# Pair products handed to TensorE beside the chain's stages, transposed in place: a linear-attention scan with a MoE on one core

## The chip, the cores and the metric

One core of a Trainium2 chip runs the whole program in one launch. The metric is the time of one execution on the device in microseconds; the kernel before was timed in three runs. A profile is of one more execution.

## What is computed

The reference is a recurrence over 768 steps for 32 heads (4 batches of 8) with a 40 x 40 state, whose output goes through a two-layer network:

```python
for t in range(S):
    y[:, :, t] = np.einsum('bhd,bhde->bhe', rt, state)
    Sa = np.einsum('bhde,bhe->bhd', state, at)
    state = state * wt[..., None] - np.einsum('bhd,bhe->bhde', Sa, bt) + np.einsum('bhd,bhe->bhde', vt, kt)
x = y.transpose(0, 2, 1, 3).reshape(3072, 320)
h = x @ w_in                       # 320 x 2048
g = np.where(h >= 1, h, np.where(h <= -1, 0.0, (h + 1) ** 2 / 4))
out = g @ w_out                    # 2048 x 320
```

All of it is in float32.

## The kernel before, in words

The scan is done in 24 chunks of 32 steps, with all 32 heads at once, in two half-batches of 16 heads (`hb`). Four chunks make a set, so there are six sets, 0 to 5. A chunk needs four things that don't depend on the state: decayed rows of k, a and b (the preparation, key `rows`, function `prelude`, L241), the products of the rows of a with the rows of b in the chunk, 32 x 32 for each head (the pair products, key `ab`, function `ab_set`, L312), the inverse of a triangular matrix made of these (key `inv`, function `invert`, L348, 31 steps of two GpSimd instructions), and score products (L478). The chain (`chain`, L504) then takes the state through the chunk, in four stages: products L519; products L529 with the inverse; products L545 and L556; products L585. Each stage is evicted by ScalarE or VectorE before the next can run.

Behind the chain the MoE (`moe`, L628) works on groups of 64 steps: products L637 (first layer), a gate on ScalarE and VectorE (L647 to L653) with a remainder on GpSimd (L654), products L668 (second layer).

The schedule is manual: each engine runs its instructions in the order in which this program issues them. A chunk has four slots. In each, the stages of the chain that are due are issued first (stage 3 of one half-batch and stage 1 of the next in the first and third slot; stage 4, stage 2 and then scores in the second and fourth), and then `fill` (L917) is called. `fill` makes six steps; in each it issues MoE work (`feed`, L901), then weight conversion, then background work (`background`, L411). The position `now` grows by 2.5 per slot, so by 10 per chunk: chunk c begins at position 10 c.

Background work is `rows`, `ab` and `inv` of the next sets. Each is a Python generator that issues some instructions and yields a number of budget units. `WINDOWS` (L28) gives from and to which position a set is worked on. `background` spreads the set's size (a sum of its yields) over its window, with the first of each two slots getting 1.4 shares and the second 0.6 (`SHARE`, L37), and advances the generator until the units spent reach the share. When a window of `inv` begins, `drain` issues what is left of the set's `ab`. Sets 0 and 1 are made in another way at the start; the generator does sets 2 to 5.

`ab_set` works on a chunk of rows in `tiab` (or, in set 2, by turns in a part of `lw` and `tiab`). `load_rows` (L298, DMAs at L304 on SP's queue) fetches it from DRAM; `shift_rows` (L306, two ScalarE copies, L310) moves the last 8 of 40 columns to other partitions; VectorE transposes 32 x 32 blocks into a tile `ea` of 8 head pairs, that is half of the chunk (L325, two instructions per half); TensorE makes 16 products for this half (L336), each recorded as two instructions; ScalarE copies the 128 x 128 result from PSUM to `pairs` (L343). `AB_W` (L41) holds the units yielded behind these steps: 6 behind the shift, 26 ahead of the products, 6 ahead of the copy, 3 behind it, 8 between chunks and 30 behind a first load. The next chunk's load is issued behind the second half's transposes. `psum()` gives one of four PSUM buffers, which the chain, the scores and the pair products share: a first write to one waits for the last eviction from it.

Of the kernel before, what the change touches and what calls it, by code (L numbers as in the profile page):

```python
# [9 lines left out]
F32 = mybir.dt.float32  # L10
# [13 lines left out]
O_R, O_V, O_K, O_P, O_A, O_B = 0, 40, 80, 120, 160, 200  # L24
# [2 lines left out]

WINDOWS = dict(  # L28
    rows=[(0, 0), (24, 43), (46, 64), (70, 90), (106, 130)],
    ab=[(0, 0), (44, 55), (68, 84), (95, 119), (135, 159)],  # L30
    inv=[(2, 28), (55.5, 79), (85, 118), (121, 158), (161, 198)],
)

# [4 lines left out]
SLOTS = len(SHARE)  # L38

ROWS_W = (2, 2, 4, 2, 6, 6, 8)  # L40
AB_W = (6, 26, 6, 3, 8, 30)  # L41
INV_W = 12
INV_STEP = [0.45 + (j + 1) * (31 - j) / 256 for j in range(31)]

# [11 lines left out]
def rwkv_moe_kernel(ctx: ExitStack, tc: tile.TileContext, r, k, v, w, a, b, w_in, w_out, ident_d, mask_d, out):  # L56
    nc = tc.nc
# [10 lines left out]
    psum = lambda: psa.tile([128, 512], F32, tag="p2", name="p2", bufs=4)  # L68
# [29 lines left out]
    work = ctx.enter_context(tc.tile_pool(name="work", bufs=1))  # L98
# [14 lines left out]
    pairs_f = pairs.rearrange("p m i -> p (m i)")  # L113
# [184 lines left out]
    def load_rows(dst, c, off, n, h0=0, nh=NH):  # L298

        sc = scr[c // 4]  # L300
        for f in range(2):
            row = (h0 + f) * 128 + 32 * (c % 4)
            src = bass.AP(sc.tensor, sc.offset + row * RW + off, [[RW, 32], [256 * RW, nh // 2], [1, n]])
            nc.sync.dma_start(dst[64 * f : 64 * f + 32], src)  # L304
# [7 lines left out]
    def ab_set(s):  # L312

        bufs = [lw[:, 0:1280].rearrange("p (h x) -> p h x", x=80), tiab] if s == 2 else [tiab]
        for c in range(4 * s, 4 * s + len(bufs)):
            load_rows(bufs[c % len(bufs)], c, O_A, 80)
            yield AB_W[5]
        for c in range(4 * s, 4 * s + 4):
            shift_rows(bufs[c % len(bufs)])
            yield AB_W[0]  # L320
            tv = bufs[c % len(bufs)].rearrange("p h (j x) -> p h j x", x=40)[:, :, :, 0:32]
            for half in range(2):
                ea = work.tile([128, 8, 2, 32], F32, tag="ea", name="ea")
                for i in range(2):
                    nc.vector.transpose(ea[:, 4 * i : 4 * i + 4], tv[:, 8 * half + 4 * i : 8 * half + 4 * i + 4])  # L325
                    yield 1
                if half and c + len(bufs) < 4 * s + 4:
                    load_rows(bufs[c % len(bufs)], c + len(bufs), O_A, 80)
                yield AB_W[1]
                ps = psum()[:, 0:128]  # L330
                for p in range(8):
                    for f in range(2):
                        rows = slice(64 * f, 64 * f + D)
                        q = 2 * f + p % 2
                        sl = p // 2
                        nc.tensor.matmul(  # L336
                            ps[32 * q : 32 * q + 32, 32 * sl : 32 * sl + 32],
                            lhsT=ea[rows, p, 0, :], rhs=ea[rows, p, 1, :], start=True, stop=True,
                        )
                yield AB_W[2]  # L340
                assert s - 1 in turned_in
                at = 256 * (c % 4) + 128 * half
                nc.scalar.copy(pairs_f[:, at : at + 128], ps)  # L343
                yield AB_W[3]
            if c < 4 * s + 3 and len(bufs) == 1:
                yield AB_W[4]

    def invert(s):  # L348

# [22 lines left out]
    def adopt(s):  # L372
# [3 lines left out]
        nc.vector.transpose(tinv.rearrange("p c h i -> p i (c h)"), W.rearrange("p (a i) -> p i a", i=32))  # L376
        turned_out.add(s)

    def staged(key, needs, work_of):
        for s in range(2 if key != "inv" else 0, NS):  # L380
            if needs:
                drain(needs, s)
            total = 0
            for d in work_of(s):
                total += d
                yield d
            if s:
                size[key] = total
            done[key] = s
            yield 0  # L390

    turned_in, turned_out = set(), set()
    done, size, spent = dict(rows=1, ab=1), dict(rows=10 + 4 * (1 + sum(ROWS_W)), ab=2 * AB_W[5] + 4 * AB_W[0] + 8 * (2 + sum(AB_W[1:4])), inv=INV_W + 2 * sum(INV_STEP)), {}
    back = {k: staged(*a) for k, a in dict(
        rows=("rows", None, prelude), ab=("ab", "rows", ab_set), inv=("inv", "ab", invert)).items()}

    def drain(key, s):

        while done.get(key, -1) < s:
            next(back[key])  # L400
# [464 lines left out]
    at = lambda n, f: todo.setdefault(n, []).append(f)  # L865
# [17 lines left out]
    i = 0  # L883
# [27 lines left out]
    def catch_up():  # L911

        for f in deferred:
            f()
        deferred.clear()

    def fill():  # L917

        catch_up()
        for k in range(6):  # L920
            feed(1280)
            if first:
                first.pop(0)()
            due[0] += PACE[now[0] >= 20]
            while due[0] > 0:
                pull(wgen)
                due[0] -= 1
            background(now[0] + 10 / SLOTS * (k + 1) / 6)
        now[0] += 10 / SLOTS
# [89 lines left out]
```

## Time and profile before

| | |
|---|---|
| median of 3 runs | 791.98 us (785.94 to 795.64) |
| the profiled execution | 791.32 us |
| its span in the trace | 789.5 us |
| busy: TensorE, VectorE, ScalarE, GpSimd | 680.1, 590.6, 472.6, 449.7 us |
| mean granted clock of TensorE | 0.907 |

The span reaches from the first instruction of the program to the last. TensorE has two rows: PE for products, PEld for weight loads, which overlap. DVE is VectorE, ACT ScalarE, POOL GpSimd, SP the engine that issues most DMAs. A line such as L336 is a line of the kernel above. The granted clock is the share of full speed that the chip let TensorE have; 1.00 and 0.50 are the two levels seen.

### The profile page before, as it was taken

To read this page: it belongs to the slowest core of one execution; us is meant where nothing else is said; L and a number is where in the kernel's file an instruction comes from. 1 tells how busy PE (TensorE), PEld (TensorE's weight loads), DVE (VectorE), ACT (ScalarE), POOL (GpSimd) and SP (SyncE) were. 2 spreads that over 40 slices of the span, in tenths; PEclk is the share of its full clock that TensorE was granted. 3 is DMA by queue.
4 is the path that set the end of the run, shared out by engine and by line. 5 is a ranking of instruction groups with operands and counts; after the bars stand their busy time and mean duration, and the time that the engine had idled before them with its cause. 6 is when DMAs were issued, how large, how long until landed. Compare 5 with 4: busy or idle time off the path is not lost.

```text
span 789.5 us, 35564 instructions
## 1 busy us (share of the span) xinstructions
PE 680.1 (86%) x15360; PEld 626.2 (79%) x15360; DVE 590.6 (75%) x1329; ACT 472.6 (60%) x1016; POOL 449.7 (57%) x615
## 2 busy tenths in 40 slices
PE   4635756688899888899989899999999999999997
PEld 4624645677778777789978889899999999999996
DVE  6998988699678686878778887688877787776211
ACT  5636755576465565557557575574765656655544
POOL 1242899866236998557758686554566642222332
PEclk9775566799689999799999999999999999999999
DMA  8898976876776666576348573442433324330100
GB/s 299 224 233 171 208 163 163 224 178 167 158 169 154 150 145 142 135 180 144 87 91 193 151 186 70 110 92 53 103 74 88 73 64 93 73 86 20 34 23 18
DMA packets 180524, 102.35 MB, mean 130 GB/s; under 512 B 124760, under 2 KB 172056, under 8 KB 180368
## 3 DMA queue, kind: packets, MB, share of 16 engines
q1 hardware_dynamic: 175216, 83.53, 47.2%
q0 software_dynamic: 4992, 16.39, 7.3%
q8 instruction: 121, 1.98, 1.1%
q14 instruction: 35, 0.29, 0.1%
q10 hardware_dynamic: 160, 0.16, 0.1%
HBM read 70.88 MB, written 27.53 MB: 125 GB/s over the span
## 4 chain that ended last, share of the span: by engine, by line
PE 61%; DVE 12%; POOL 10%; issue 6%; ACT 6%; DMA 4%; SPq 0%; POOLq 0%; ACTq 0%; DVEq 0%
PE ph L637 20%; PE po L668 18%; PE p L556 5%; PE p L545 3%; PE p L585 3%; PE p L485 3%; PE p L519 3%; PE p L529 3%; POOL lw L369 2%; POOL lw L363 2%; DMA scr<-arena 2%; POOL w L772 2%; PE p L336 1%; DMA tiab<-scr 1%; POOL gl L654 1%
## 5 line engine op out<-in xcount | busy, mean ns | idle before, releaser
L637 PE MATMUL ph<-X,w 120*128 120x256 f32 x1536 | 224.7, 301 | 5.1 <-DMA X<-Y 3.7
L654 POOL TENSOR_TENSOR gl<-gt,gh 128x512 fp32r<-128x512 f32 x95 | 122.1, 1285 | 163.8 <-ACT gh L653 156.9
L637 PEld LDWEIGHTS ph<-X,w 120*128 120x128 f32 x1536 | 203.1, 202 | 12.7 <-issue 3.0
L668 PE MATMUL po<-w,gh 128*128 128x320 f32 x768 | 135.7, 319 | 8.4 <-ACT gh L653 7.8
L650 DVE SCALAR_TENSOR_TENSOR gt<-gt,ph 128x512 f32<-128x512 f32 x95 | 65.0, 685 | 94.0 <-ACT gt L648 85.8
L668 PEld LDWEIGHTS po<-w,gh 128*128 128x128 f32 x768 | 118.4, 195 | 10.7 <-ACT gh L653 9.2
L653 ACT CAST gh<-gt 128x512 fp32r<-128x512 f32 x95 | 58.8, 619 | 85.1 <-DVE gt L650 75.5
L647 ACT ACTIVATE gt<-ph,half_c 128x512 f32<-128x512 f32 x95 | 65.2, 687 | 54.6 <-PE ph L637 53.8
L369 POOL TENSOR_TENSOR lw<-lw 128x31 f32<-128x31 f32 (+15 forms) x155 | 88.9, 573 | 8.4
L363 POOL TENSOR_TENSOR lw<-lw 128x31 f32<-128x31 f32 (+15 forms) x155 | 87.1, 562 | 8.0
L563 DVE SCALAR_TENSOR_TENSOR cg<-p,pr 40x160 f32<-40x160 f32 x184 | 59.1, 321 | 34.0 <-PE p L556 31.7
L668 PE MATMUL po<-w,gl 128*128 128x320 f32 x384 | 75.2, 318 | 10.5 <-POOL gl L654 10.5
L497 DVE TENSOR_TENSOR cg<-p,mask 32x256 f32<-32x256 f32 x192 | 80.5, 419 | 4.4 <-PE p L485 0.9
L540 ACT ACTIVATE cg<-p 32x160 f32<-32x160 f32 x192 | 56.5, 295 | 38.0 <-DVE cg L536 24.3
L668 PEld LDWEIGHTS po<-w,gl 128*128 128x128 f32 x384 | 61.1, 192 | 13.6 <-POOL gl L654 13.4
L556 PE MATMUL p<-cg 128*64 128x72 f32 (+1 forms) x1536 | 64.5, 242 | 0.0
L576 POOL TENSOR_TENSOR Y<-yt,Y 128x256 fp32r<-128x256 f32 x48 | 36.0, 750 | 49.1 <-ACT Y L575 49.0
L536 DVE SCALAR_TENSOR_TENSOR cg<-p,mask 32x128 f32<-32x128 f32 x192 | 55.2, 288 | 9.5 <-ACT cg L540 3.9
L648 ACT ACTIVATE gt<-gt 128x512 f32<-128x512 f32 x95 | 60.0, 632 | 3.0
L556 PEld LDWEIGHTS p<-cg 128*64 128x64 f32 x1536 | 58.9, 151 | 0.4 <-issue 0.4
L545 PEld LDWEIGHTS p<-cg 128*40 128x40 f32 x1472 | 36.0, 130 | 21.5 <-ACT cg L540 13.4
L545 PE MATMUL p<-cg 128*40 128x40 f32 x1472 | 42.2, 218 | 12.5 <-ACT cg L540 12.5
(105 smaller groups left out, 1103.1 us busy)
## 6 DMA issues: line engine op xcount, KB each, us to landing
ti<-scr SPq DMA_DIRECT2D x96, 200.0 KB
scr<-arena POOLq DMA_DIRECT2D x16, 640.0 KB, 5.4
cg<-scr SPq DMA_DIRECT2D x96, 80.0 KB
X<-Y SPq DMA_DIRECT2D x36, 160.0 KB
scr<-wide SPq DMA_DIRECT2D x8, 640.0 KB
w<-in_moe_w_out_dram SPq DMA_DIRECT2D x16, 320.0 KB
tiab<-scr SPq DMA_DIRECT2D x28, 160.0 KB
cg<-scr SPq DMA_DIRECT2D x96, 40.0 KB
```

The source lines that it names most:

```text
L363: eng.tensor_mul(t3, W3[:, 0:n, j : j + 1].broadcast_to([128, n, m]), L3[:, j + 1 :, j].unsqueeze(1).broadcast_to([128, n, m]),)
L369: eng.tensor_sub(W3[:, 0:n, j + 1 :], W3[:, 0:n, j + 1 :], t3)
L497: nc.vector.tensor_tensor(out=cg[q, f::2, C_X : C_X + 64][:, 4 * i : 4 * i + 4].rearrange("p h (j x) -> p h j x", x=32), in0=ps[quarter(f, ...
L545: nc.tensor.matmul(pst[er[h % 2], h // 2, :], lhsT=cg[:, h, C_S : C_S + D], rhs=cg[:, h, C_G : C_G + D], start=True, stop=True)
L556: nc.tensor.matmul(psv[h // 8][64 * f : 64 * f + 64, h // 2 % 4, 0:n3], lhsT=cgw[:, h * CW + C_G : h * CW + C_G + 64], rhs=cg[:, h, C_R : ...
L563: nc.vector.scalar_tensor_tensor(out=cn[er[f], f::2, C_S : C_S + D][:, halves[i]], in0=psv[i][er[f], :, 32:72], scalar=-1.0, in1=pr[er[f], ...
L637: nc.tensor.matmul(phs[k % 2][:, n * j : n * j + n], lhsT=wt[0, f // 4, wi // 2][:, wi % 2, fs], rhs=Xs[g][:, xi, :], start=i == 0, stop=i ...
L647: nc.scalar.activation(gt, ph, AF.Relu, bias=half_c, scale=0.5)
L648: nc.scalar.activation(gt, gt, AF.Square)
L650: nc.vector.scalar_tensor_tensor(out=gt, in0=gt, scalar=1.0, in1=ph, op0=ALU.min, op1=ALU.max)
L654: nc.gpsimd.tensor_sub(gl, gt, gh.bitcast(F32))
L668: nc.tensor.matmul(pos[i], lhsT=x[:, ts_], rhs=w, start=q == 0 and k == 0, stop=end)
```

## The change

A chunk is now handled as a whole. Four transposes write back to where they read. The chunk's 32 products are put into a function `multiply`, which goes on a list `beside`; `flush` runs what is on the list, and each `fill` begins with it, behind the stages of the slot. The generator then yields single units until the products have been issued, at most 45, and runs `flush` itself if they haven't been by then. One copy of 128 x 256 evicts them. The next load of the same buffer is issued behind that copy, with 44 units (2 in set 2) before the next shift. `ab_size` gives the planner a size with 18 to 20 units of waiting per chunk. The window of set 3 moves from (68, 84) to (66.5, 84.5).

```diff
-    ab=[(0, 0), (44, 55), (68, 84), (95, 119), (135, 159)],
+    ab=[(0, 0), (44, 55), (66.5, 84.5), (95, 119), (135, 159)],
-AB_W = (6, 26, 6, 3, 8, 30)
+AB_W = (4, 10, 6, 3, 3, 30, 44)
+AB_WAIT = 45
@@ ab_set @@
-            for half in range(2):
-                ea = work.tile([128, 8, 2, 32], F32, tag="ea", name="ea")
-                for i in range(2):
-                    nc.vector.transpose(ea[:, 4 * i : 4 * i + 4], tv[:, 8 * half + 4 * i : 8 * half + 4 * i + 4])
-                    yield 1
-                if half and c + len(bufs) < 4 * s + 4:
-                    load_rows(bufs[c % len(bufs)], c + len(bufs), O_A, 80)
-                yield AB_W[1]
-                ps = psum()[:, 0:128]
-                for p in range(8):
+            for i in range(4):
+                hs = slice(4 * i, 4 * i + 4)
+                nc.vector.transpose(tv[:, hs], tv[:, hs])
+                yield AB_W[4]
+            yield AB_W[1]
+            products = []
+
+            def multiply():
+                ps = psum()[:, 0:256]
+                for h in range(16):
                     for f in range(2):
                         rows = slice(64 * f, 64 * f + D)
-                        q = 2 * f + p % 2
-                        sl = p // 2
+                        q = 2 * f + h % 2
+                        sl = h // 2
                         nc.tensor.matmul(
                             ps[32 * q : 32 * q + 32, 32 * sl : 32 * sl + 32],
-                            lhsT=ea[rows, p, 0, :], rhs=ea[rows, p, 1, :], start=True, stop=True,
+                            lhsT=tv[rows, h, 0, :], rhs=tv[rows, h, 1, :], start=True, stop=True,
                         )
-                yield AB_W[2]
-                assert s - 1 in turned_in
-                at = 256 * (c % 4) + 128 * half
-                nc.scalar.copy(pairs_f[:, at : at + 128], ps)
-                yield AB_W[3]
-            if c < 4 * s + 3 and len(bufs) == 1:
-                yield AB_W[4]
+                products.append(ps)
+
+            beside.append(multiply)
+            for _ in range(AB_WAIT):
+                if products:
+                    break
+                yield 1
+            else:
+                flush()
+            yield AB_W[2]
+            assert s - 1 in turned_in
+            nc.scalar.copy(pairs_f[:, 256 * (c % 4) : 256 * (c % 4) + 256], products[0])
+            yield AB_W[3]
+            if c + len(bufs) < 4 * s + 4:
+                load_rows(bufs[c % len(bufs)], c + len(bufs), O_A, 80)
+                yield AB_W[6] if len(bufs) == 1 else 2
+
+    beside = []
+
+    def flush():
+
+        for f in beside:
+            f()
+        beside.clear()
@@ staged @@
+    def ab_size(s):
+        each = AB_W[0] + 4 * AB_W[4] + sum(AB_W[1:4])
+        return 2 * AB_W[5] + 4 * (each + 20) + 4 if s == 2 else AB_W[5] + 4 * (each + 18) + 3 * AB_W[6]
...
-                size[key] = total
+                size[key] = ab_size(s + 1) if key == "ab" else total
@@ fill @@
         catch_up()
+        flush()
         for k in range(6):
             feed(1280)
```

## Rows read from the trace of the kernel before

**Rows 1.** The page: busy time by engine; products and clock in 40 slices.

```profile
PE 680.1 (86%) x15360; PEld 626.2 (79%) x15360; DVE 590.6 (75%) x1329; ACT 472.6 (60%) x1016; POOL 449.7 (57%) x615
...
PE   4635756688899888899989899999999999999997
...
PEclk9775566799689999799999999999999999999999
```

**Rows 2.** Chunks 4-11, 14, 15, 17: stretch, length, busy PE PEld DVE ACT POOL, PEclk.

```profile
178.38:218.82 40.44, 33.58 (x660) 30.24 (x657) 31.74 (x65) 22.21 (x49) 16.03 (x18) 0.79 0.73 162
218.82:252.32 33.50, 31.11 (x724) 27.69 (x720) 26.82 (x60) 20.14 (x46) 16.53 (x19) 0.90 0.61 149
252.32:283.43 31.11, 26.95 (x565) 24.32 (x561) 21.63 (x50) 17.87 (x39) 28.87 (x45) 0.95 0.73 171
283.43:320.93 37.50, 30.69 (x723) 28.03 (x720) 28.70 (x66) 21.69 (x48) 33.15 (x49) 0.91 0.63 135
320.93:353.36 32.43, 29.64 (x661) 26.61 (x657) 27.82 (x56) 17.68 (x38) 14.55 (x17) 0.89 0.66 161
353.36:378.34 24.98, 24.98 (x595) 23.29 (x593) 20.34 (x51) 17.68 (x40) 20.09 (x34) 1.00 0.59 128
378.34:407.31 28.97, 27.65 (x660) 25.57 (x656) 20.65 (x52) 16.13 (x37) 16.55 (x23) 0.94 0.46 102
407.31:440.39 33.08, 28.39 (x692) 25.61 (x688) 28.15 (x63) 21.78 (x49) 29.03 (x40) 0.96 0.71 162
...
491.76:518.79 27.03, 26.32 (x660) 24.19 (x656) 19.77 (x50) 15.70 (x37) 15.21 (x21) 1.00 0.47 103
518.79:545.30 26.51, 26.51 (x693) 24.43 (x689) 20.31 (x52) 18.19 (x43) 16.05 (x27) 1.00 0.39 78
...
569.68:594.10 24.42, 24.42 (x565) 22.90 (x561) 18.08 (x45) 15.45 (x35) 16.73 (x25) 1.00 0.33 70
```

**Rows 3.** Groups by line, 178 to 545 us.

```profile
L325 DVE STREAM_TRANSPOSE ea<-tiab 128x256 f32<-128x256 f32 x56 | 21.0, 410 | 4.9 <-ACT tiab L310 3.6 <-PE p L336 1.3
...
L336 PE MATMUL p<-ea 40*32 40x32 f32 x1024 | 16.4, 202 | 11.7 <-DVE ea L325 6.7 <-DVE cg L587 2.4 <-DVE yt L568 1.6
...
L485 PE MATMUL p<-cg,ev 40*32 40x32 f32 x768 | 11.3, 199 | 4.4 <-ACT pairs L343 3.8 <-DVE ev L467 0.7
...
L523 ACT COPY x<-p 128x288 f32<-128x288 f32 x24 | 9.6, 400 | 12.5 <-PE p L519 12.2
...
L343 ACT COPY pairs<-p 128x128 f32<-128x128 f32 x32 | 8.4, 264 | 17.2 <-PE p L336 17.2
```

**Rows 4.** Waits of TensorE and ScalarE: total us, times, longest us.

```profile
PE p L336 <- DVE ea L325: 6.7, 5, 3.6
...
PE p L336 <- ACT ss L550: 0.9, 1, 0.9
...
ACT tiab L310 <- DMA tiab<-scr: 5.7, 6, 2.1
...
ACT lw L310 <- DMA lw<-scr: 4.4, 2, 4.1
```

**Rows 5.** Short stretches around waits: columns as in Rows 2.

```profile
202.20:215.90 13.70, 12.72 (x253) 11.56 (x254) 10.99 (x24) 7.61 (x19) 4.18 (x4) 0.50 0.79 158
294.40:297.80 3.40, 3.40 (x33) 3.34 (x21) 3.26 (x9) 2.60 (x7) 3.32 (x5) 0.50 1.02 207
...
410.00:413.00 3.00, 1.89 (x43) 1.88 (x44) 2.93 (x9) 2.66 (x8) 2.81 (x3) 1.00 0.26 61
```

**Rows 6.** Timeline at two starts of a fill: start us, length us, instruction.

```profile
209.57 0.63 PE L485 MATMUL p<-pr,ev 40*32 40x32 f32 x32
...
210.28 0.83 DVE L587 SCALAR_TENSOR_TENSOR cg<-p,pr 40x256 f32<-40x256 f32 x2
...
282.88 0.85 ACT L550 COPY ss<-p 40x320 f32<-40x320 f32 x2
...
283.43 0.71 PE L519 MATMUL p<-cg 128*32 128x72 f32 x32
```

More of the change, by code (lines that the diff above doesn't have):

```diff
@@ L392, in rwkv_moe_kernel @@
     turned_in, turned_out = set(), set()
-    done, size, spent = dict(rows=1, ab=1), dict(rows=10 + 4 * (1 + sum(ROWS_W)), ab=2 * AB_W[5] + 4 * AB_W[0] + 8 * (2 + sum(AB_W[1:4])), inv=INV_W + 2 * sum(INV_STEP)), {}
+    done, size, spent = dict(rows=1, ab=1), dict(rows=10 + 4 * (1 + sum(ROWS_W)), ab=ab_size(2), inv=INV_W + 2 * sum(INV_STEP)), {}
     back = {k: staged(*a) for k, a in dict(
```

## The prediction

> **What bounds the kernel now.** I read the page first. TensorE is busy 680 of 789.5 us, and the line of 40 slices shows where it isn't: it is short of full in slices 1 to 22 and full from there to the last ones, and the granted clock drops below 9 in the same early slices only [rows 1]. So there are two regimes. To see where they meet, I cut the trace at the start of each chunk (the place of its L519 products) and read busy time and clock by stretch [rows 2]. Chunk 17 has no pair work: 24.42 us, TensorE busy for all of it, clock 1.00. That is the floor of a chunk, set by TensorE. Chunk 9 is nearly there (24.98) though it carries preparation and an inverse. Chunks 4 to 8, 10 and 11 take 29 to 40 us, with TensorE idle for 1.3 to 7 us and the clock under 1 in each. From chunk 12 on the program runs at TensorE's pace in an order written out by hand, so whatever is won before 440 us shifts all that follows and comes out at the end one to one; what is won later is small.
>
> The pair work lies in chunks 4 to 15. Its direct price is the idle time by line: TensorE stood 11.7 us before pair products L336, of which 6.7 for ea and 4.9 for a PSUM buffer (2.4, 1.6 and 0.9), and 3.8 us before score products L485 whose buffer a pair copy L343 still held [rows 3, 4]. An indirect price follows some of these waits. The longest (3.6 us [rows 4], set 2's first product, at 203 us) is at the start of a stretch of 13.7 us at a granted clock of 0.50, in which TensorE is busy for 12.72 us; around another, at 294 us, there are 3.4 us at 0.50 [rows 5]. Half of 1.0 is the lower of the two levels (1.2 instead of 2.4 GHz), so work in such a stretch takes twice as long.
>
> **The change part by part.** All sums go against the profiled execution's own 791.32 us (span 789.5 and 1.8 around it); the median of the three runs is 791.98, 0.7 above, and their spread of 9.7 us is over 1%.
>
> *Transposes in place.* Four per chunk before, of 128x256, four after: 64 x about 0.41 us on VectorE either way [rows 3]. An output stepped by 40 is not shown for this instruction; between nothing and twice the time that is 0 to 26 us of VectorE over 367 us in which it is busy for some 80%. I take nothing. What goes is the single buffer ea, for which a transpose had to wait for the products.
>
> *Products in one group.* 32 groups of 16 products become 16 of 32. TensorE's own time for them, 16.4 us [rows 3], stays; merging saves at most the entry of 16 groups, under 2 us at the end of the sum, taken as nothing.
>
> *Where the group goes.* This is the step that counts. Before, a group is issued in the middle of a fill, between two MoE products, and its transposes a few planner units ahead: in the queue of TensorE, which runs in order, it then stands before MoE work that has everything it needs. After, a group is only put on a list, and the next fill issues it first, right behind the stages. By the planner's arithmetic (a unit of budget per yield, the window's share by slot), the groups fall at positions 47.5, 50 and 55 of set 2, 70, 75, 80 and 85 of set 3, 100, 112.5 and 120 of set 4, 140, 152.5 and 160 of set 5: thirteen at the start of a fill. Three more (52.5, 107.5, 147.5) come at the end of a fill, since the 45 units of waiting run out there. The transposes are issued 10 units and more ahead, behind them the whole chain stage, so the 6.7 us of waiting for ea should go, and with it most of the 4.9 us for PSUM.
>
> *What it costs.* The group now takes the fifth PSUM buffer of a slot when the stages have just taken four. It must wait until the first of them is evicted. At a slot with L545 to L519 ahead, the eviction L550 ended at 283.73 and L519 at 284.14: no wait. At a slot with scores ahead, L485 ended at 210.20 and the L587 that frees a buffer at 211.11: 0.9 us [rows 6]. Bounds for 13 starts: 0 and 13 x 0.9 = 12 us. Eleven of the 13 stand behind L519 and are like the first row, so I take 2 us.
>
> *One copy.* 32 copies of 0.264 us become 16; the nearest copy of that size is 128x288 in 0.40 us [rows 3]. 8.4 us become 6.4 of ScalarE, which is 60% busy [rows 1]: nothing. ScalarE's idle time before L343 (17.2 us [rows 3]) goes, since the copy follows a product that is long done; this frees the gates behind it.
>
> *Loads.* The next chunk's rows can only be loaded when the products have read them, 44 units ahead of their shift, where before it was 43: nothing on SP in sum. ScalarE waits for these rows today, 5.7 us on tiab and 4.4 on lw [rows 4], and transposes and gates queue behind it. That stays: set 2's first shift comes one step later (4.1 becomes about 3 us), set 3's first load, now at 66.7, has 1.25 positions until its shift instead of 2.1, that is 3 us at 24.4 us per ten positions, and will wait some 2. Its rows are stored by 64, so nothing else holds it.
>
> *Last copies.* In sets 2 to 5 the last copy now falls on the inverse's first step, and VectorE's transposition of pairs waits for it. ScalarE is a step behind at most: 4 x 0.5 us, on VectorE only; taken as nothing on the path.
>
> **The sum.** I work out a ceiling by chunk, as against a neighbour with the same other load [rows 2], with 0.5 us for each pair group (16.4 / 32); a group is 32 of TensorE's records, so what a chunk's count exceeds 565 by tells how many it has.
> - Chunk 4: its wait 3.6 and half of the 12.72 us at low clock: 9.9.
> - Chunk 5 against chunk 6 (31.11) and 5 groups: nothing; I grant 1.
> - Chunk 7 against chunk 6, with 5 groups: 37.50 - 31.11 - 2.6 = 3.8.
> - Chunk 8 against chunk 9 (24.98), with two groups more: 32.43 - 24.98 - 1.0 = 6.4.
> - Chunk 10 against chunk 9, two groups more: 3.0, but a new group of tokens waits for its rows there, with a drop of the clock behind: 0.
> - Chunk 11: its own waits 1.6 + 0.9 = 2.5.
> - Chunks 14 and 15 against chunk 17 with 3 and 4 groups: 1.1 and 0.1.
> Together about 25 us. How much of a removed stall comes back as another? ScalarE's 10 us of waiting for rows [rows 4] are the best candidates, two thirds of the 15.5 us that go [rows 3], and they sit just ahead of the same products. I take half: 12.5 us, less 2 for PSUM. 791.3 - 10.5 = 780.8; with the 0.7 to the median 781.5; I say 781.
>
> **The rivals.**
> *All of it comes back.* If the clock stays up behind every removed wait and the gates absorb ScalarE's waits, the ceiling counts: 791 - 25 = 766. For it: chunk 9 shows that preparation, inverse and MoE fit into 25 us. Against: chunk 6 needs 31 without any pair work.
> *The waits only move.* The group isn't in the way of the MoE products, but the shift is: ScalarE stands for the rows, the gate behind it comes late, and L668 waits for gh in the place of L336 for ea. Then only the 4.9 us for PSUM and the 3.8 before the scores go, less 2, less some 3 us for set 3's hurried load: 791 - 4 = 787 to 791. The change also does less than it says where the 45 units run out, 3 of 16.
> *The group waits for PSUM, and the clock falls.* One mechanism on the other side: at each of the 13 starts TensorE stands before the group until an eviction is through, 0.9 us as in [rows 6], and each such stop is followed by 3.4 us at half clock, which costs 1.7 [rows 5]. 13 x 2.6 = 34 us, less the 12.5: 791 + 21 = 812. It decides from about 2.2 us per start. Against it: after the wait of 1.6 us at 411 us, for just such a buffer, the clock stayed at 1.00 [rows 5], and eleven of the thirteen show no wait to come.
> The Trainium skill speaks for this last case: "TensorE: Matmul & The Clock Gate", section "A second HAM failure mode: psum-queue depth-cycling", tells of a kernel in which short stops between groups, while PSUM buffers are cycled, made the clock swing between its levels and cost throughput. By that rule the time would be this rival's 812; the row at 411 us speaks against it for stops of this length, and no run here yet shows many in a row.
>
> **How the numbers follow.** About 2% (16 us) is what a measurement of this kernel tells from no change. The forecast, 781, has 0.50, its own range being 775 to 786; all of it back, 766, has 0.22; waits only moved, 789, has 0.22; the PSUM rival, 812, has 0.06. Faster by over 2% means under 776: the second case and a fifth of the first, 0.30. Slower by over 2% means over 808: 0.04, two thirds of the last case. The rest, 0.66, is within. The range takes in the second case and the third: 765 to 795; outside are the last case and the far ends of the others.
>
> **What would show it.** Right: no wait of TensorE on ea's successor over 1 us; chunks 7 and 8 at some 33 and 28 us; no half clock from 202 to 216 us; chunk 17 unchanged at 24.4. Step by step: in-place transposes at 0.41 us; 16 copies at about 0.4; the list of waits without L485 on pairs; ScalarE's waits for tiab and lw still near 10 us. The forecast is wrong if L668's waits for gh and gl grow by what L336 loses, if L336 waits on L550 or L587 at most starts, or if half-clock stretches appear in chunks 10 to 15, which have hardly any now.

## The result and the profile after

| | before | changed |
|---|---|---|
| median of 20 runs | 791.04 us (785.45 to 798.14) | 784.06 us (775.95 to 786.13) |
| profiled execution, its span | 791.32, 789.5 us | 782.96, 780.8 us |
| mean granted clock in it | 0.907 | 0.919 |

The ratio is 0.9902, with a 95% interval of 0.9882 to 0.9922: the change is worth 1%, clear of noise and under 2%. In the changed kernel the lines have moved: transposes L325, pair products L337, their copy L352, the chain's products L541, L551, L567, L578 and L607, evictions L572 (before L550) and L609 (L587), scores L507, MoE products L659 and L690, gates L669 to L676.

The page of the changed kernel, as [rows 1]:

```profile
PE 665.7 (85%) x15360; PEld 617.2 (79%) x15360; DVE 590.4 (76%) x1329; ACT 471.1 (60%) x1000; POOL 450.1 (58%) x615
...
PE   4645756777689798789989899999999999999997
...
PEclk9865566799889899999999999999999999999999
```

TensorE is busy 14 us less than before, more than the span has lost (8.7). So in this execution it does not wait less; its work took less time. The chunks, as [rows 2], cut at the first of the L541 products (chunks 4 to 11, 14, 15, 17; the last two columns, there as here, are the busy share of the DMA engines and GB/s):

```profile
178.89:219.71 40.82, 28.89 (x628) 26.51 (x624) 31.80 (x65) 23.08 (x50) 17.32 (x19) 0.87 0.66 153
219.71:251.87 32.16, 29.11 (x756) 26.68 (x753) 26.20 (x60) 19.05 (x40) 15.44 (x18) 0.95 0.69 168
251.87:283.43 31.56, 27.65 (x564) 25.14 (x561) 22.75 (x53) 17.14 (x37) 29.24 (x46) 0.89 0.70 165
283.43:317.79 34.36, 28.47 (x692) 26.00 (x688) 25.02 (x60) 19.76 (x44) 29.59 (x40) 0.95 0.62 141
317.79:350.12 32.33, 26.37 (x692) 24.25 (x688) 28.84 (x59) 19.48 (x41) 18.27 (x24) 1.00 0.66 163
350.12:374.54 24.42, 24.42 (x565) 22.91 (x561) 20.19 (x51) 17.36 (x39) 19.54 (x34) 1.00 0.62 137
374.54:404.42 29.88, 27.76 (x691) 25.90 (x689) 22.30 (x54) 16.94 (x37) 18.82 (x24) 0.94 0.46 105
404.42:435.76 31.34, 27.46 (x629) 25.17 (x625) 26.23 (x61) 20.87 (x46) 27.71 (x38) 0.95 0.68 165
486.29:512.54 26.25, 25.83 (x692) 24.20 (x689) 19.29 (x49) 16.28 (x38) 16.33 (x22) 1.00 0.45 107
512.54:537.75 25.21, 25.21 (x627) 23.66 (x624) 20.56 (x53) 17.33 (x40) 15.54 (x27) 1.00 0.38 82
562.83:587.24 24.41, 24.41 (x564) 22.90 (x560) 18.07 (x45) 15.44 (x35) 16.73 (x25) 1.00 0.33 70
```

Chunk 7 has lost 3.1 us, chunk 11 1.7, chunks 5, 14 and 15 1.3, 0.8 and 1.3; chunk 4, of which most was hoped, is 0.4 longer, chunk 8 has lost 0.1, chunk 6 is 0.4 and chunk 10 0.9 longer. Chunk 17 is the 24.4 us that it was. From the start of chunk 4 to that of chunk 16 it is 366.9 us before and 358.9 after; in these, TensorE stood idle 31.2 us before and 37.5 after (length less busy time), and was busy 335.7 and 321.3.

Groups by line in this stretch of the changed kernel, as [rows 3]:

```profile
L659 PE MATMUL ph<-X,w 120*128 120x256 f32 x768 | 110.1, 298 | 0.8 <-issue 0.5 <-DMA X<-Y 0.2
...
L690 PE MATMUL po<-w,gh 128*128 128x320 f32 x384 | 67.0, 318 | 8.9 <-ACT gh L675 8.9
...
L325 DVE STREAM_TRANSPOSE tiab<-tiab 128x256 f32<-128x256 f32 x56 | 19.9, 409 | 8.4 <-ACT tiab L311 8.4
...
L337 PE MATMUL p<-tiab 40*32 40x32 f32 x832 | 10.6, 196 | 8.2 <-ACT ss L572 6.3 <-DVE yt L590 1.7 <-issue 0.2
...
L352 ACT COPY pairs<-p 128x256 f32<-128x256 f32 x15 | 5.6, 374 | 4.6 <-PE p L337 4.6
...
L337 PE MATMUL p<-lw 40*32 40x32 f32 x128 | 2.0, 217 | 7.1 <-DVE cg L609 7.1
```

And two groups of the kernel before in the same stretch, which stand in no row above:

```profile
L637 PE MATMUL ph<-X,w 120*128 120x256 f32 x768 | 116.5, 307 | 1.3 <-DMA ti<-scr 1.3
...
L668 PE MATMUL po<-w,gh 128*128 128x320 f32 x384 | 70.0, 324 | 4.3 <-ACT gh L653 4.3
```

The MoE products L637 and L668 became L659 and L690, in the same number. One of the first took 307 ns before and 298 after, of the second (with gh) 324 and 318: together 9.4 us less, with no edit to either. Most of this is the clock: over the stretch the granted share is 0.93 before and 0.96 after, and in chunk 9, where it is 1.00 in both, one of the first takes 289 ns before and after. One of the second takes 313 and 310 ns there, so about 1 us of the 9.4 is not the clock. The pair products took 16.4 us and take 12.6 for 15 of the 16 groups (the last, some 0.8 us more, falls behind the stretch's end). Transposes in place took 409 ns, as before 410. Half the copies, at 374 ns, took 5.6 us instead of 8.4.

The two profiled executions show more of the clock than the other runs do. The changed kernel's had the second highest of its 20 runs (0.902 to 0.920); their mean is 0.911. The kernel before, timed again beside the experiments, had 0.909 over 54 runs (runs more than 1.5% above the fastest of their kernel are left out). The share of the clock that was not granted, times the span, is 73.4 us before and 63.2 after in the profiled pair, but 71.6 and 69.7 on average over these runs, whose mean span fell by 7.2 us. By this estimate the clock accounts for some 2 us of the 7, by the spread of the runs between none and 4; what makes up the rest in a run at the usual clock, no trace here shows.

Waits of TensorE, as [rows 4] (gh is the gate's output, written by ScalarE; gl is its remainder, by GpSimd):

```profile
PE po L690 <- ACT gh L675: 12.8, 11, 2.2
PE po L690 <- POOL gl L676: 12.0, 6, 4.4
...
PE p L337 <- DVE cg L609: 7.1, 1, 7.1
PE p L337 <- ACT ss L572: 6.3, 3, 2.1
```

No wait for the transposes is left. But the group waits for PSUM: 7.1 us once for L609, 6.3 for L572 and 1.7 for L590, 15 us instead of the 4.9 of before. And L690 waits 12.8 and 12.0 us for gh and gl, where L668 waited 7.8 and 10.5. The longest wait, in order of time (start, length, instruction, idle before it):

```profile
202.01 0.40 ACT L311 COPY lw<-lw 32x256 f32<-32x256 f32 x1 [4.08 <-DMA lw<-scr]
...
203.37 1.42 DVE L325 STREAM_TRANSPOSE lw<-lw 128x256 f32<-128x256 f32 x4 [3.63 <-ACT lw L311]
...
204.75 0.69 DVE L672 SCALAR_TENSOR_TENSOR gt<-gt,ph 128x512 f32<-128x512 f32 x1
...
208.05 1.45 DVE L236 TENSOR_TENSOR_SCAN wz<-wz,dz 128x400 f32<-128x400 f32 x1
...
209.42 0.83 DVE L609 SCALAR_TENSOR_TENSOR cg<-p,pr 40x256 f32<-40x256 f32 x2
...
210.51 1.20 PE L337 MATMUL p<-lw 40*32 40x32 f32 x64 [7.14 <-DVE cg L609]
```

Set 2's first rows are late. ScalarE stands 4.1 us for them at its shift, and VectorE 3.6 us at the transposes, which are queued ahead of L609, the eviction that frees a PSUM buffer. Behind the transposes VectorE then has 4.6 us of gate and preparation (L672 to L236) to do before L609, so the late rows are only part of this delay. The group is issued at the start of the next fill, behind the scores, and stands in TensorE's queue for 7.1 us. At this place TensorE had stood 3.6 us for ea before the change.

What the clock did around three such waits (columns as in [rows 2]; the first stretch lies in the long wait and behind it, the others hold a wait of 2.1 us each):

```profile
206.90:217.20 10.30, 6.69 (x88) 6.66 (x89) 8.51 (x19) 5.27 (x13) 3.49 (x4) 0.50 0.75 150
300.00:304.00 4.00, 2.61 (x74) 2.58 (x75) 3.06 (x9) 2.36 (x6) 3.62 (x5) 0.81 0.18 38
319.00:323.00 4.00, 2.43 (x78) 2.39 (x79) 3.93 (x9) 2.86 (x6) 3.57 (x5) 1.00 0.26 79
```

From 206.9 us, within the wait of 7.1 us, the clock was at its lower level for 10.3 us, 3.6 of them in the wait; around the first wait of 2.1 us it fell for part of the stretch, around the second not at all, nor around the third (1.00 from 336.5 to 340.5 us).

### The profile page after: what moved, and what is told of

It reads as the page before. It is cut to its first block, busy times and chain, and to the rows that moved or that the text cites. A ratio compares the mean times of both kernels' runs of the same rounds, so it can differ in the third digit from the quotient of the medians.

```text
span 780.8 us, 35565 instructions
## 1 busy us (share of the span) xinstructions
PE 665.7 (85%) x15360; PEld 617.2 (79%) x15360; DVE 590.4 (76%) x1329; ACT 471.1 (60%) x1000; POOL 450.1 (58%) x615
## 4 chain that ended last, share of the span: by engine, by line
PE 55%; POOL 11%; DVE 11%; ACT 7%; DMA 7%; issue 6%; SPq 2%; POOLq 0%; ACTq 0%; DVEq 0%
PE ph L659 19%; PE po L690 16%; PE p L578 4%; DMA scr<-arena 4%; POOL lw L381 3%; PE p L567 3%; PE p L607 3%; POOL lw L387 3%; PE p L541 2%; PE p L507 2%; PE p L551 2%; DMA X<-Y 2%; POOL gl L676 1%; POOL w L794 1%; DMA tiab<-scr 1%
## 5 line engine op out<-in xcount | busy, mean ns | idle before, releaser
L659 PE MATMUL ph<-X,w 120*128 120x256 f32 x1536 | 218.3, 297 | 5.2 <-DMA X<-Y 4.6
L676 POOL TENSOR_TENSOR gl<-gt,gh 128x512 fp32r<-128x512 f32 x95 | 122.0, 1284 | 159.0 <-ACT gh L675 157.4
L659 PEld LDWEIGHTS ph<-X,w 120*128 120x128 f32 x1536 | 198.9, 199 | 11.8 <-issue 4.8
L690 PE MATMUL po<-w,gh 128*128 128x320 f32 x768 | 131.9, 314 | 13.4 <-ACT gh L675 12.8
L672 DVE SCALAR_TENSOR_TENSOR gt<-gt,ph 128x512 f32<-128x512 f32 x95 | 65.0, 684 | 87.7 <-ACT gt L670 79.6
L690 PEld LDWEIGHTS po<-w,gh 128*128 128x128 f32 x768 | 116.8, 192 | 16.0 <-ACT gh L675 15.1
L669 ACT ACTIVATE gt<-ph,half_c 128x512 f32<-128x512 f32 x95 | 65.2, 686 | 55.6 <-PE ph L659 54.8
L690 PE MATMUL po<-w,gl 128*128 128x320 f32 x384 | 74.7, 317 | 12.0 <-POOL gl L676 12.0
L519 DVE TENSOR_TENSOR cg<-p,mask 32x256 f32<-32x256 f32 x192 | 80.5, 419 | 5.0 <-PE p L507 1.5
L690 PEld LDWEIGHTS po<-w,gl 128*128 128x128 f32 x384 | 60.8, 191 | 15.2 <-POOL gl L676 15.2
L578 PE MATMUL p<-cg 128*64 128x72 f32 (+1 forms) x1536 | 64.5, 242 | 0.0
L578 PEld LDWEIGHTS p<-cg 128*64 128x64 f32 x1536 | 58.9, 151 | 0.4 <-issue 0.4
L567 PEld LDWEIGHTS p<-cg 128*40 128x40 f32 x1472 | 36.2, 130 | 21.8 <-ACT cg L562 13.7
L567 PE MATMUL p<-cg 128*40 128x40 f32 x1472 | 42.4, 218 | 12.5 <-ACT cg L562 10.3
```

The lines of the kernel that those rows point to most:

```text
L519: nc.vector.tensor_tensor(out=cg[q, f::2, C_X : C_X + 64][:, 4 * i : 4 * i + 4].rearrange("p h (j x) -> p h j x", x=32), in0=ps[quarter(f, ...
L567: nc.tensor.matmul(pst[er[h % 2], h // 2, :], lhsT=cg[:, h, C_S : C_S + D], rhs=cg[:, h, C_G : C_G + D], start=True, stop=True)
L578: nc.tensor.matmul(psv[h // 8][64 * f : 64 * f + 64, h // 2 % 4, 0:n3], lhsT=cgw[:, h * CW + C_G : h * CW + C_G + 64], rhs=cg[:, h, C_R : ...
L659: nc.tensor.matmul(phs[k % 2][:, n * j : n * j + n], lhsT=wt[0, f // 4, wi // 2][:, wi % 2, fs], rhs=Xs[g][:, xi, :], start=i == 0, stop=i ...
L669: nc.scalar.activation(gt, ph, AF.Relu, bias=half_c, scale=0.5)
L672: nc.vector.scalar_tensor_tensor(out=gt, in0=gt, scalar=1.0, in1=ph, op0=ALU.min, op1=ALU.max)
```

## The experiments

Each kernel was timed against the kernel before in five rounds on the same chip. There were three sessions of four kernels, each on another chip, so kernels of different sessions are compared by their ratios.

**The place of the group.** Issued by the generator in mid-fill, as it was before, with all else as changed (called the mid-fill variant below):

```diff
-            beside.append(multiply)
-            for _ in range(AB_WAIT):
-                if products:
-                    break
-                yield 1
-            else:
-                flush()
+            for _ in range(20):
+                yield 1
+            multiply()
```

> The changed kernel, but the generator issues the whole chunk's group itself, 20 units behind the transposes, in the middle of a fill; transposes in place, one group, one copy and the window stay. Theory (place): the gain goes, 789 to 792 us, 0.998 to 1.002; waits before the group move back to the transposes and PSUM, and L507 waits for pair copies again. Rival (one group and one copy in place are what helps, wherever they stand): 783 to 786 us, 0.990 to 0.993.

Measured: 780.84 us, ratio 0.9897 (0.9862 to 0.9932). The rival is right: the list and `flush` earn nothing over a generator that issues the same group itself. By the planner's arithmetic these groups stand at 47.5, 50.4, 52.1 and so on, some in the middle of a fill and some at its edges; those of set 3 stand at 70.8, 75.4, 80.0 and 85.4, beside the same slots as in the changed kernel (70, 75, 80, 85). So this run tests the list and not which slot a group meets. Over the stretch TensorE is idle for 31.0 us, as before (31.2), and the clock is at 0.96.

**Set 3's window put back.**

```diff
-    ab=[(0, 0), (44, 55), (66.5, 84.5), (95, 119), (135, 159)],
+    ab=[(0, 0), (44, 55), (68, 84), (95, 119), (135, 159)],
```

> The changed kernel with set 3's window put back to (68, 84); nothing else differs. Theory (the gain is the place of the group): the window is worth little, some 784 to 786 us, 0.991 to 0.993 of the kernel before; chunks 7 and 8 together within 2 us of the changed kernel's 66.7. Rival (the earlier window of set 3 made the gain, as chunk 7 is where most of it shows): 788 to 790 us, 0.997 and more, with chunk 7 back at 37 us.

Measured: 792.42 us, 1.0021 (0.999 to 1.0053). All of the gain is gone, a little more than the rival had it: chunk 7 takes 38.4 us and chunk 8 36.9, together 75.3 instead of 66.7. The wait that grew is

```profile
PE p L507 <- DVE cg L609: 11.9, 6, 4.9
```

against 1.6 us in the changed kernel; 10.1 us of it are three waits in chunks 7 and 8. TensorE's idle time over the stretch is no longer than in the changed kernel (36.1 against 37.5 us); the clock is at 0.93 instead of 0.96, and over all runs at 0.903 instead of 0.911. With this window the 45 units run out for set 3, and its groups stand at the end of the fills before 72.5, 77.5 and 82.5, each ahead of a slot with scores. The score products want a PSUM buffer and must wait for L609. Chunk 15 has then no room left: its shift, transposes, products and copy are issued in one burst at 85.4. To see if the end of the fill is to blame, the same with more waiting:

```diff
-    ab=[(0, 0), (44, 55), (66.5, 84.5), (95, 119), (135, 159)],
+    ab=[(0, 0), (44, 55), (68, 84), (95, 119), (135, 159)],
-AB_WAIT = 45
+AB_WAIT = 200
```

> The changed kernel with set 3's window put back to (68, 84) and up to 200 units of waiting instead of 45, so that no group is issued at the end of a fill: those of set 3 stand at the starts 72.5, 77.5 and 82.5, behind the scores, and the last is issued in one burst at 85.4. Theory (a group at the end of a fill holds one of four PSUM buffers through the next stages, which is what the old window cost): the waits of L507 for L609, 12 us there, fall under 5, and the time is 783 to 786 us. Rival (the burst of chunk 15 and the missing room cost it): 788 to 792 us.

Measured: 797.96 us, 1.0101 (1.0064 to 1.0138), slower than before and outside both ranges. In set 3 the wait for L609 has not gone, it has moved to the group:

```profile
PE p L337 <- DVE cg L609: 20.4, 5, 7.5
```

Of the 20.4 us, 11.8 are the three groups of set 3; 7.5 are the wait of set 2's first group, which the changed kernel has too (7.1). Chunks 7 and 8 take 74.7 us, as with the ends of fills (75.3). So it isn't the end of a fill. In set 3, a slot with stage 4 and scores that has a group beside it must wait until VectorE has done L609: the scores do where the group stands ahead of the stages, the group where it stands behind them. (In sets 4 and 5 the changed kernel has two groups behind scores, at 112.5 and 152.5, and neither waits.) That the run is slower still is another matter: with 200 units the groups of sets 4 and 5 move too, the last of each to the start of the inverse's window, and chunks 12 and 16 grow by 5.5 and 2.3 us. The burst of chunk 15 is in both runs with the list and the old window, so what it costs is not tested. The window at 66.5 puts set 3's groups at 70, 75, 80 and 85, behind L541, where a buffer is freed by ScalarE's L572.

**The window alone, in the old form and in the mid-fill variant.**

```diff
-    ab=[(0, 0), (44, 55), (68, 84), (95, 119), (135, 159)],
+    ab=[(0, 0), (44, 55), (66.5, 84.5), (95, 119), (135, 159)],
```

> The kernel before with set 3's window alone moved to (66.5, 84.5). With the old window put back, the changed kernel lost all of its gain. Theory (window by itself: the work of set 3 had too little room in its 16 positions, whatever its form): 782 to 785 us, 0.988 to 0.993, with chunks 7 and 8 at 67 us or less instead of 70. Rival (window and new form belong together: the old window only hurts where the group runs into the ends of fills and chunk 15 is issued in one burst): 788 to 792 us, 0.996 to 1.002.

Measured: 794.56 us, 1.0052 (1.002 to 1.0083): by itself the window does harm. Chunks 7 and 8 take 68.4 us in its profile, 1.5 less than before; chunks 6 and 11 are 3.7 us longer each. And the mid-fill variant with the old window (its edit is that of the second experiment):

> The mid-fill variant (group issued by the generator 20 units behind the transposes) with set 3's window put back to (68, 84). Its groups of set 3 then stand at 71.7, 75.8, 80.4 and 85.4. Theory (window by itself): back to 789 to 792 us. Rival (the form, one group transposed in place, makes the gain, and the old window hurt only the group that waits for a fill): 781 to 785 us, 0.989 to 0.993.

Measured: 784.91 us, 0.9923 (0.9893 to 0.9953), not to be told from 0.9897 with the new one. Its groups of set 3 also stand behind the slots 70, 75, 80 and 85, and chunk 15's shift and transposes are issued at 82, with no burst of all its work at the end. The window is worth nothing of its own. It is needed where groups wait for fills, as it decides which slots they meet.

**Which part of the form.** First two PSUM buffers and two copies, the products in the same place:

```diff
-                ps = psum()[:, 0:256]
+                ps = None
                 for h in range(16):
+                    if h % 8 == 0:
+                        ps = psum()[:, 0:128]
+                        products.append(ps)
...
-            nc.scalar.copy(pairs_f[:, 256 * (c % 4) : 256 * (c % 4) + 256], products[0])
+            for i in range(2):
+                at = 256 * (c % 4) + 128 * i
+                nc.scalar.copy(pairs_f[:, at : at + 128], products[i])
```

> The mid-fill variant with the chunk's products in two PSUM buffers of 16 products each and two copies of 128x128, issued where the one group and the one copy stood. Theory (one copy and one buffer are worth nothing by themselves): within its noise of the mid-fill variant, 780 to 784 us, 0.987 to 0.993. Rival (half as many copies and buffers held is what helps): 787 to 791 us, 0.996 to 1.001.

Measured: 790.96 us, 1.0000 (0.9971 to 1.0028). The theory fails: with two buffers the whole gain is gone, though every product stands where it stood. By line in the stretch, first the mid-fill variant, then this one:

```profile
L574 PE MATMUL p<-cg 128*64 128x72 f32 x771 | 30.3, 232 | 0.0
...
L547 PE MATMUL p<-x,tinv 32*32 32x72 f32 x768 | 17.6, 228 | 1.0 <-issue 0.5 <-DVE tinv L390 0.4
...
L537 PE MATMUL p<-cg 128*32 128x72 f32 x768 | 17.1, 230 | 2.1 <-ACT ss L568 2.1
...
L503 PE MATMUL p<-cg,ev 40*32 40x32 f32 x768 | 11.1, 197 | 4.7 <-DVE cg L605 2.9 <-ACT pairs L348 1.1 <-DVE ev L485 0.7
...
L337 PE MATMUL p<-tiab 40*32 40x32 f32 x832 | 10.6, 196 | 5.3 <-ACT ss L568 3.4 <-PE po L686 1.0 <-DVE yt L586 0.9
```

```profile
L578 PE MATMUL p<-cg 128*64 128x72 f32 x772 | 31.3, 234 | 4.6 <-ACT ss L572 3.0 <-ACT pairs L352 1.0 <-DVE cg L519 0.6
...
L551 PE MATMUL p<-x,tinv 32*32 32x72 f32 x768 | 18.4, 228 | 6.7 <-DVE cg L609 4.2 <-ACT pairs L352 1.1 <-issue 0.9
...
L507 PE MATMUL p<-cg,ev 40*32 40x32 f32 x768 | 11.1, 197 | 2.0 <-DVE cg L558 1.3 <-DVE ev L489 0.7
...
L340 PE MATMUL p<-tiab 40*32 40x32 f32 x832 | 10.5, 196 | 3.5 <-ACT ss L572 2.4 <-PE po L690 1.0
```

The pair products don't wait longer than in the mid-fill variant. It is the chain's own products that now do, L578 and L551 for 4.6 and 6.7 us where they waited 0.0 and 1.0 (there they are L574 and L547): pair work holds two of the four buffers, and a stage must wait for an eviction. In part this is the mid-fill variant's own wait at another place: its scores L503 and its L537 stood 4.0 and 2.1 us for a buffer, where this run's scores L507 stand 1.3 and its L541 doesn't wait for an eviction. In sum TensorE's waits for a PSUM buffer in the stretch go from some 10 to some 13 us; another 3.5 us before L541 end at nothing that the profile shows. Over the stretch TensorE is idle for 37.7 us against 31.0, and the clock is at 0.94 against 0.96 (over all runs 0.908 against 0.914). So the run shows what two buffers and two copies cost together; that it is the buffers and not the second copy is argued from these waits. Then the halves through ea, with one buffer and one copy:

```diff
-            for i in range(4):
-                hs = slice(4 * i, 4 * i + 4)
-                nc.vector.transpose(tv[:, hs], tv[:, hs])
-                yield AB_W[4]
+            for half in range(2):
+                ea = work.tile([128, 8, 2, 32], F32, tag="ea", name="ea")
+                for i in range(2):
+                    nc.vector.transpose(ea[:, 4 * i : 4 * i + 4], tv[:, 8 * half + 4 * i : 8 * half + 4 * i + 4])
+                    yield AB_W[4]
+                for _ in range(15):
+                    yield 1
...
```

> The mid-fill variant with the chunk again in two halves through the single tile ea of before: two transposes, 15 units, 16 products, and the same for the second half; one PSUM buffer and one copy at the end, and the units per chunk as in the mid-fill variant. Theory (what helps is that the whole chunk's transposes are far ahead of the one group, so that TensorE waits for ea once per chunk at most): the waits for ea come back, 5 to 7 us, and the time is 787 to 791 us, 0.995 to 1.001. Rival (the pace helps: how the units of a chunk are spread, and that less is left for the end of a window): 780 to 784 us.

Measured: 793.33 us, 1.0046 (1.0008 to 1.0083). As the theory said, the waits for ea are back, and more than it said:

```profile
L338 PE MATMUL p<-ea 40*32 40x32 f32 x992 | 16.6, 203 | 20.5 <-DVE ea L327 15.5 <-DVE cg L601 4.9
```

Neither part alone gives the gain: one copy with the products in two halves, or the products in one place with two buffers and copies, has the time of before or somewhat more. The halves differ in two more things, though. Their products stand 15 units behind their transposes, where it was 26 before, and the one buffer is held from the first half to the second. So the split itself is not told apart from these.

**What is late next.** The list issued behind the first step of MoE work:

```diff
         catch_up()
-        flush()
         for k in range(6):
             feed(1280)
+            if k == 0:
+                flush()
```

> The changed kernel with the list issued behind the fill's first step of MoE work instead of ahead of it. TensorE stood 15 us before the group for a PSUM buffer whose eviction was late. Theory (that wait is on the path, since the MoE work behind it had all it needs): the wait falls under 5 us and the time by 4 to 8, 776 to 780 us. Rival (the evicting engines are late anyway, and TensorE only meets them one instruction later, at L690 for gh or at the next stage): 783 to 786 us, and the waits for gh and gl grow by what the group's wait loses.

Measured: 783.61 us, 0.9908 (0.9878 to 0.9939), as the changed kernel. The group's waits for PSUM fall from 15.1 to 7.7 us, and L690's for gh rise from 12.8 to 15.2: the rival, for the time. A third of the removed wait shows there, and TensorE's idle time over the stretch falls by 1.3 us only (37.5 to 36.2). Next the loads of rows left out, as its expectation says:

```diff
-                load_rows(bufs[c % len(bufs)], c + len(bufs), O_A, 80)
```

> The changed kernel without the load of the second to fourth chunk of rows in a set (third and fourth in set 2): the pair products of these chunks are made of the rows that lie there. Shift, transposes, products and copy stay, and no shift waits for rows but each set's first. Theory (ScalarE and VectorE standing for rows make the evictions late): ScalarE's wait on tiab falls from 2.7 to about 1 us, VectorE's on the shift from 12 to 5, the 2.1 us waits before the group in set 3 shrink, and the time falls by 4 to 8 us, 776 to 780. Rival (the rows' waits are covered by other work): 783 to 785 us.

Measured: 784.13 us, 0.9927 (0.9899 to 0.9955). ScalarE's wait for tiab fell to 1.0 us, but VectorE's for the shift hardly did (8.4 us in the changed kernel):

```profile
DVE tiab L325 <- ACT tiab L311: 7.9, 3, 4.1
```

So VectorE does not stand there for the rows, but for a ScalarE that comes late for another reason. The list of ScalarE's waits of the changed kernel names one:

```profile
ACT arena L273 <- DMA scr<-arena: 28.9, 8, 6.8
```

`arena` is the buffer in which the preparation puts its rows together before they are stored: it writes the next part where the last part is still being stored. Before the change this wait was 12.4 us (the wait at the same copy for VectorE's scan fell meanwhile from 16.9 to 12.8). The store sooner:

```diff
-ROWS_W = (2, 2, 4, 2, 6, 6, 8)
+ROWS_W = (2, 2, 4, 2, 3, 3, 14)
```

> The changed kernel with six units moved from ahead of the store of prepared rows to behind it (6, 6, 8 become 3, 3, 14). ScalarE stood 28.9 us for that store, as its next copy writes the same buffer. Theory (this is the wait that is late next and keeps evictions and gates late): ScalarE's wait falls below 20 us, the waits of L690 for gh below 8, and the time is 778 to 781 us. Rival (it is covered, or GpSimd's products come late for the rows of b instead): 783 to 786 us.

Measured: 779.72 us, 0.9868 (0.983 to 0.9906). ScalarE's wait for the store and L690's wait for gh are small now, and VectorE's for the shift of tiab fell from 8.4 to 4.3 us. But the same copy now waits 19.3 us for VectorE's scan instead of 12.8, so its two waits fall together from 41.7 to 25.6, and the wait for gl, GpSimd's, has grown by 7:

```profile
ACT arena L273 <- DVE ld_w L236: 19.3, 10, 3.4
...
ACT arena L273 <- DMA scr<-arena: 6.3, 3, 2.2
```

```profile
PE po L690 <- POOL gl L676: 19.3, 8, 5.4
...
PE po L690 <- ACT gh L675: 3.3, 4, 1.2
```

The interval overlaps that of the changed kernel, so the gain of some 4 us over it is likely, not settled.

**A version to beat both.** The sooner store with the mid-fill variant, and with the changed kernel where set 2 alone is issued in mid-fill:

> The mid-fill variant with the store of prepared rows sooner (3, 3, 14 units), which gave 0.987 with the changed kernel. Theory (the two are independent, one in the pair work's form, one in ScalarE's wait for the store): 775 to 779 us, 0.981 to 0.986. Rival (both remove the same lateness, so they don't add): 779 to 783 us.

Measured: 781.93 us, 0.9884 (0.9842 to 0.9927), in the rival's range: no sign that the two add, though the interval reaches into the theory's range as well.

```diff
+            if s == 2:
+                for _ in range(20):
+                    yield 1
+                multiply()
+            else:
+                beside.append(multiply)
```

> The changed kernel with the sooner store of rows, and set 2 alone issued by the generator in mid-fill, as its first group stood 7 to 8 us for a PSUM buffer at the start of a fill behind the scores. Theory (that wait is on the path): 774 to 778 us, 0.979 to 0.985, and chunk 4 some 3 us shorter than with the sooner store alone. Rival (the chunk is late for its rows anyway): 779 to 782 us, chunk 4 unchanged.

Measured: 778.08 us, 0.9844 (0.9803 to 0.9885), the lowest of all. The group's wait for L609, 8.0 us with the sooner store alone, is gone from its list; half of it (3.9 us) has moved to the scores, which now wait for the same eviction (here L614):

```profile
PE p L512 <- DVE cg L614: 4.7, 3, 3.9
```

Chunk 4 took 34.4 us in its profile and 36.0 with the sooner store alone, but chunk 5 took 33.3 and 29.7. So the gain over the sooner store alone (0.9868) is neither clear of noise nor seen where the theory had put it. The version is faster than the kernel before by 1.2 to 2.0%; its interval and that of the changed kernel just meet.

## Why the prediction was right, and where it was not

The time, 784.06 us, lies in the range and 3 us from the forecast. The way there was another, so that it came so near is in part luck: the sum had TensorE wait less, and in the profiled pair it waits 6.3 us more, while its busy time falls by 14.4. The terms one by one:

- *Transposes in place* at nothing: right, 409 ns and 410.
- *Products in one group* at nothing: 3 us less (16.4 to some 13.4), where I had allowed for under 2.
- *The waits for ea go*: right, none is left, nor do the scores wait for a pair copy any more. The run with halves through ea brought back 15.5 us of them and had no gain; as its products also stood nearer to their transposes, this fits the term and does not prove it.
- *Where the group goes, "the step that counts"*: half wrong. The list earns nothing; issued in mid-fill the same group gives 0.9897. But which slot a group meets does count: with set 3's groups beside scores all of the gain is gone (1.0021).
- *One copy, "nothing"*: wrong. I priced a copy by ScalarE's time, 2 us, and did not ask what a group holds. With two buffers and two copies per chunk the ratio is 1.0000.
- *The PSUM wait, 2 us*: the largest miss, 15.1 us. I had taken one row for a slot behind L519 and one behind scores [rows 6] as typical, with eviction engines as punctual as before. (By my own list ten of the 13 starts stand behind L519, not eleven: 47.5, 112.5 and 152.5 stand behind scores.) At 47.5 it was 7.1 us, as VectorE had the transposes of late rows, a gate and preparation ahead of L609; in set 3 it was 2.1 us three times, as ScalarE came late to L572.
- *What is late next, half of 25 us*: the name was wrong. I named ScalarE's waits for tiab and lw, 10 us; they are 7.3 now, and without most of the loads the time is the same. Its waits for the store of arena grew from 12.4 to 28.9, and TensorE's for gh and gl from 18.3 to 24.8. That is 6.5 us, about what the pair products lost in waits for ea (6.7): the first of the signs that I had given for a wrong forecast came.
- *The clock*: I took half-clock stretches behind the removed waits as part of the ceiling. The one from 202 to 216 us, whose absence was to show me right, is still there from 206.9 to 217.2. In the profiled pair the gain does show at the clock, in most of the 9.4 us of the MoE products; over all runs the clock accounts for some 2 us of 7, and the rest is open. That the clock goes with the long waits was read from rows; no run here sets it by itself.
- *By chunk*: chunk 7 should have come to some 33 us and has 34.4; chunk 8 should have come to 28 and has 32.3, with two of the three 2.1 us waits in it. Chunk 4's 9.9 us did not come at all.
- *The window*: I gave it a price, a wait of 2 us at set 3's first load. Alone it does harm (1.0052). For groups that wait for a fill it decides which slots they meet.
- *Readings*: 0.22 and a fifth of 0.50 are 0.32, not 0.30, for a time under 776 us. Slice 23 of the page is also short of full (8 tenths), so the first regime reaches a little further than slice 22.

Of the rivals, the one with PSUM and the clock was half true. The waits came, 15 us against the 12 of its bound, but the clock fell for 10.3 us at the longest and not behind each. "The waits only move" was true of much of the waiting (those for gh and gl grew, and the later `flush` moved a wait without changing the time) but not of the sum: 784 us is below its 787. The rule that I cited from the Trainium skill ("TensorE: Matmul & The Clock Gate", "A second HAM failure mode: psum-queue depth-cycling") is about short stops that come often. Of the three stops of 2.1 us in set 3 one had a drop of the clock beside it and two had none, and the stop of 7.1 us is not a short one. So for these stops the trace does not bear the rule out, and no run here shows many in a row.

## What to carry to other kernels

Where several users share a few PSUM buffers, price a group by the buffers that it holds and by which engine frees them, not by the time of its copy alone; two buffers and two copies instead of one cost 1% here. Before you place work by a planner, look up which stage each placement meets: the same groups gave 1% beside one stage and nothing beside another. And in a kernel whose TensorE is not full, compare busy time per product as well as waits, and the clock of the profiled execution with that of the other runs: one profile can show more of the clock than the gain holds.

## What the runs showed that I had not expected

In the profiled pair TensorE's idle time rose by 6 us while the program became 8 us faster, as its products ran longer at the upper clock (0.96 instead of 0.93 of full over chunks 4 to 15); by the clock of the other runs this is not the whole of the gain. And a change of planner constants alone, a store issued six units sooner, took ScalarE's wait for it from 28.9 to 6.3 us, though over a quarter of this came back at the same copy as a wait for VectorE.
